# Two attention and two feed-forward layers on one core: gate and up weights on two queues, other weights behind them, wider fillers, another order

## The chip, the cores and the metric

The kernel runs on one core of one Trainium2 chip. The metric is the device time of one execution in microseconds (us). Engines named here: PE (TensorE, matrix multiplication), DVE (VectorE), ACT (ScalarE), POOL (GpSimd) and SP (SyncE, which here only issues transfers). Each engine runs its own list of instructions in order and waits on semaphores for the others. Transfers are issued from SP's list and from ACT's; the issue takes a place in that list, the data is moved by 16 DMA engines.

## The reference

A sequence of 2,048 tokens with 448 features, bf16, goes through four layers: attention, feed-forward, attention, feed-forward, each added to its input after a layer norm without weights. The same weights serve both pairs of layers.

```python
def _A_ref(x, wqkv, wo):            # 16 heads of 28
    W, dil = 8, 2
    q, k, v = ...                    # x @ wqkv
    idx = pos[:, None] - (jnp.arange(W) * dil)[None, :]   # 8 keys: own, and every second one before
    mask = idx >= 0
    logits = jnp.einsum("bhsd,bhswd->bhsw", q, kg) * scale
    attn = _softmax(jnp.where(mask, logits, -1e9))
    return einsum("bhsw,bhswd->bhsd", attn, vg) @ wo
def _B_ref(x, w_gate, w_up, w_down): # 448 -> 1792 -> 448, no nonlinearity
    return ((x @ w_gate) * (x @ w_up)) @ w_down
x = x + _A_ref(_layernorm(x), A_wqkv, A_wo)
x = x + _B_ref(_layernorm(x), B_w_gate, B_w_up, B_w_down)
# both lines once more
```

## The kernel before

x stays in SBUF (`x_sb`), 16 blocks of 128 tokens. The tokens are dealt to the blocks by parity, so that a step of two in the sequence is a step of one within a half. Work is cut into chunks of 256 or 512 tokens; a chunk of a layer is a job, and `SEQ` (line 77) lists the jobs: A00 is chunk 0 of attention layer 0, B10 chunk 0 of feed-forward layer 1, A2x and B3x are the second pair. Jobs of different layers overlap.

A chunk of attention: `ln_chunk` (771) computes bn_stats, the variance's logarithm and exponential on ACT, and the normalised block `xn_sb`. In layer 0 PE transposes it (line 812, copied to `xnTa` in line 818); in the later layers a DMA transpose on SP's queue does (805). `qk_chunk` (872) multiplies by `WQK` and copies the result to `qk` (904); four features per head group go through DRAM by seven small writes (913, `vt`) and come back by transposing loads (924), for all but the first tokens of layer 0. `v_group` (926) makes V. `attn_front` (1002) makes the scores (1016), their exponential (1023) and the mask (1033); `attn_back` (1041) multiplies by V (1053), and its result is evacuated (1064, 1068) and normalised (1078 to 1091). `y_blocks` (1095) multiplies by `wo_g` and `x_block` adds to x (1108).

A chunk of feed-forward, `b_chunk` (1118): for each of 14 column groups, seven steps with gate weights on partitions 0 to 63 and up weights on 64 to 127 of `WGU` side by side, a copy of the gate result on ACT (1144), the product on DVE (1147); then `WD` (twin_blocks, and 1159 for the last blocks) and the add. Nearly all matmuls are recorded by one helper and carry line 539, or 542 where four narrow strips replace a whole one, so that they can run between the matmuls of an attention product.

The order of each engine's list is not written by hand. `Sched` (136) takes every operation with an estimated duration, dependencies and a priority and simulates a list scheduler; what comes out is the order, and the waits are put in from it. Priorities are made of a job's place, of numbers per kind of operation (`PR`, `XP`) and per job (`JP`), and of `HEAD_P` for the first normalisations. `HOLD_A`, `HOLD_BA` and `HOLD_BB` say how long attention bursts are held back. `LINE_T`, `LINE_T2` and `LINE_W` are its assumption on how long PE takes to get 256 instructions. None of these numbers is on the chip; they change the order alone.

The first loads go out by `head_dma`: blocks of x on SP's queue, wqkv rows (into `hT`, used as a stage) on both. Until data is there PE multiplies zeros (line 705): `WARM` = 9 pairs of 512 columns, then `FILL` = 33 pairs of 256 with the lowest priority, which go wherever nothing else is ready. After the third group of x has landed (`BULK_AFTER`, the key ("x", -1, 8)) the bulk weights follow, all on SP's queue, by `bulk` (732): four loads of wo, eight of gate and up in turn (two halves of the columns, each in pieces of 4 and 3 of the 7 row groups, `KP`), and four of wd, the first after an evacuation of the first attention product, each other after the landing of the one before.

Of the kernel before, what the change touches and what calls it, by code (L numbers as in the profile page):

```python
# [27 lines left out]
MAIN = "R64"  # L28
# [2 lines left out]
MAXALT = 2  # L31
PE_T = ("00", "01", "02", "03", "04")
HEAD_LN = 5
HEAD_P = (-9741.69, -21156.5, 9471.13, 16516.09, 9510.52)
HOLD_A = 10125.5
HOLD_BA = 5146.2
HOLD_BB = 35088.1
HOLD_N = 2
S_EST = 288.0
AV_EST = 288.0  # L40
# [6 lines left out]
VT = 4  # L47
# [5 lines left out]
AVC = True  # L53
AVC_E = ("act", "dve")
NBK = 8
PR = {'AV': -13607.23, 'rstd': -12825.88, 'bn': -7069.68, 'N': -625.26, 'Gps': 7235.74, 'Tps': 2822.91, 'H': -12368.72, 'S': -4010.55, 'VT': 5090.9, 'Ex': 7210.49, 'G': 2122.84, 'xn': -11304.9, 'QK': 896.52, 'Ddps': 1031.01, 'V': 3968.38, 'x': 577.18, 'lnv': 7.22, 'Oc': 7676.01, 'Oa': -2117.27, 'R': 11367.91, 'VVps': -11282.71, 'Yps': -6204.95, 'PW': 15173.02, 'T': -4657.77, 'mv': -9765.28, 'Rs': 6778.63, 'Rl': -11802.58, 'QKps': -3286.81, 'E': -6014.8, 'wqk': -7832.24, 'wqp': 1681.38}
JP = {'A20': -5129.89, 'B32': -1640.88, 'B34': -20489.15, 'A22': -2226.98, 'B13': -11980.33, 'A21': -2482.24, 'B12': -12384.07, 'A02': 5531.08, 'A03': -2969.67, 'B30': -18200.21, 'B31': -1620.52, 'B10': -8375.7, 'B11': -7187.21, 'A23': -3100.22, 'A04': -7074.05, 'B33': 9501.01, 'A01': 4103.52, 'B14': -535.73, 'A00': 22844.77}
OFF = {}
XP = {'bn': -5669.71, 'mv': -13506.16, 'lnv': 1000.78, 'rstd': 5707.23, 'xn': 4967.8, 'Tps': -6347.24, 'T': -10883.81, 'QK': -8329.91, 'V': -3666.67, 'E': 818.94, 'Ex': -6364.37, 'S': -9748.38, 'AV': -5394.24, 'Oc': 7335.77, 'Oa': 10978.51, 'N': 720.48, 'x': -8291.39, 'VT': 14228.52, 'PW': 1447.12}
VONES_L = 6000.0  # L60
BL = (8000.0, 8000.0, 4800.0)
WOL = 3500.0
KP = ((0, 4), (4, 7))
BULK_Q = "sp"
BULK_WD = [("Oc", 0, 0, 0)]
BULK_AFTER = [("x", -1, 8)]
PAIR_PLAIN = (7, 7)
ACH = {0: (256, 512, 512, 512, 256), 2: (512, 512, 512, 512)}
BCH = {1: (256, 512, 512, 512, 256), 3: (256, 512, 512, 512, 256)}
WARM = 9  # L70
FILL = 33
SEED = 190
JITTER = 0
ATT_P = 17045.15
A_CAP = 6
B_CAP = 6
SEQ = "A00 A01 B10 A02 B11 A03 A04 B12 A20 B13 A21 B14 B30 A22 B31 A23 B32 B33 B34".split()
# [58 lines left out]
class Sched:  # L136
# [26 lines left out]
    def add(self, engs, ins, est, deps=(), prio=0.0, mode=None, acquire=None, release=(), dma=None, lat=0.0, after=None, selfd=(), tmin=None, alt=()):  # L163
# [78 lines left out]
    def run_pe(self, now, n, stream):  # L242

        n0 = self.fed[-1][0]
        t = now
        if self.fed[-1][1] < now:
            self.fed.append((n0, now))
        lead = min(self.QUEUE, (now - self.fed_at(n0, self.QUEUE)) / self.FETCH)
        end = now + stream
        if n > lead:  # L250
            end = max(end, now + (n - lead) * self.FETCH + self.REFILL)
        while len(self.lines) * self.LINE <= n0 + n + self.AHEAD:
            k = len(self.lines)
# [6 lines left out]
            self.lines.append(at + (self.LINE_T2 if self.LINE_W[0] <= at < self.LINE_W[1] else self.LINE_T))  # L260
# [25 lines left out]
    def schedule(self):  # L286
# [29 lines left out]
        while left:  # L316
            moved = False
            b_ready = any(o.acquire is not None and o.acquire.kind == 1 for o in pend["pe"])
            for e in self.ENGS:
# [28 lines left out]
                if okay and e == "pe":  # L348
# [219 lines left out]
def build(nc, A_x, A_wqkv, A_wo, B_w_gate, B_w_up, B_w_down, out):  # L568
# [52 lines left out]
    def one(fn, key=None):  # L621
        return [(fn, key)]
# [5 lines left out]
    def plain_dma(q, dst, src, key, sem, deps=(), lat=3000.0, prio=0.0, tmin=None):  # L628
        sc.add(q, one(lambda E: E.dma_start(dst, src), key), {"sp": 520.0, "act": 500.0, "pool": 1000.0}[q], deps=deps, dma=sem, mode=0, lat=lat, prio=prio, tmin=tmin)
# [72 lines left out]
    wb = Banks(2)  # L702
    fill = None
    for n in range(WARM + FILL):
        ins = [(lambda E, h=h, c=512 if n < WARM else 256: E.matmul(ps[:, wb[h], 0:c], warm[64 * h:64 * h + 64, 0:128], warm[64 * h:64 * h + 64, 0:c], start=True, stop=True), ("warm", n) if h else None) for h in range(2)]  # L705
# [21 lines left out]
    ones_dst = vt_all.rearrange("(t e) (a n) -> t e a n", e=32, n=128)[:, DH:32]  # L727
    ones_src = ones32[0:32, :].unsqueeze(1).to_broadcast([32, 16, 128])
    plain_dma("sp", ones_dst, ones_src, ("vones",), "d_one", deps=["c_ones"], lat=VONES_L, prio=-40)
    chain = []  # L730

    def bulk(dst, src, key, sem, lat):
        late = key[0] == "wd"
        deps = BULK_WD if late and key[1] == 0 else [chain[-1]] if late else BULK_AFTER
        plain_dma(BULK_Q, dst, src, key, sem, deps=["c_wo"] + deps, lat=lat, prio=-50.0 + len(chain) * 0.1)
        chain.append(key)

    for j in range(4):
        dst = wo_g[32 * j:32 * j + DH, :, :]
        src = A_wo.rearrange("(c j e) d -> j e c d", c=4, j=4, e=DH)[j]  # L740
        bulk(dst, src, ("wo", j), f"d_wo{j}", WOL)
    for n in range(2):
        f0, f1 = F // 2 * n, F // 2 * (n + 1)
        for m, (a, z) in enumerate(KP):
            for w, W_ in enumerate((B_w_gate, B_w_up)):
                bulk(WGU[64 * w:64 * w + 64, a:z, f0:f1], W_[64 * a:64 * z, f0:f1].rearrange("(k p) f -> p k f", p=64), (("wg", "wu")[w], n, m), f"d_w{'gu'[w]}{n}{m}", BL[0])
    for n in range(4):
        f0, f1 = (0, 4, 7, 11, 14)[n:n + 2]
        bulk(WD[:, f0:f1, :], B_w_down[128 * f0:128 * f1, :].rearrange("(c p) e -> p c e", p=128), ("wd", n), f"d_wd{n}", BL[2])
    WDR = [("wd", n) for n in range(4)]  # L750
    WO = [("wo", j) for j in range(4)]

# [365 lines left out]
    def b_chunk(li, j, n_b, prio):  # L1118
# [65 lines left out]
    def a_chunk(li, j, prio):  # L1184
# [105 lines left out]
```

## Time and profile before

| | |
|---|---|
| median of 3 runs (lowest, highest) | 392.72 us (392.54, 394.02) |
| profiled execution | 392.95 us |
| its span, first to last instruction | 391.2 us |
| PE busy | 381.8 us, 98% of the span |
| DVE, ACT busy | 272.8 us (70%), 204.6 us (52%) |
| granted TensorE clock | 1.000 |

The span is the time between the first and the last instruction of the profiled execution; 1.75 us of its time lie outside. In rows of the timeline stand the start and duration in us, the engine, the line of the kernel, the operation, the tiles written and read with their shapes, and the count; brackets give the idle time before it and what ended it. "PEld" is the loading of a matmul's weights, "SPq" and "ACTq" are transfers issued from these lists. In rows by stretch of time stand the length, then busy time and number of instructions for PE, PEld, DVE, ACT and POOL, then the granted clock, the share of time in which the 16 DMA engines are busy, and GB/s. Rows of transfers have their number, KB each and the median us from issue to landing. "issue" as a releaser means that the engine waited for nothing that the profile shows.

### The profile page before, as it was taken

Reading aid. Unit: us, or ns where it says so; the run is one execution under the profiler, and the core shown is the slowest. Engines: PE = TensorE matmul, PEld = TensorE weight load, DVE = VectorE, ACT = ScalarE, POOL = GpSimd, SP = SyncE. Lnnn points to the kernel's source line nnn. Section 1 sums busy time; section 2 is a strip of 40 time slices with the busy share of each in tenths; the row PEclk is TensorE's granted clock in tenths of the full one; section 3 lists DMA queues with packets and bytes.
Section 4 is the critical chain, followed back from the end, with each engine's and each line's share of the span. In section 5 each row is a group of like instructions: output and inputs, shape, how many; then the busy total and the mean of one; then the engine's idle time right before and its main releaser. Section 6 shows DMA issues by size and latency. Waiting matters only on the chain.

```text
span 391.2 us, 14452 instructions
## 1 busy us (share of the span) xinstructions
PE 381.8 (98%) x6416; PEld 215.3 (55%) x6416; DVE 272.8 (70%) x597; ACT 204.6 (52%) x394; POOL 8.9 (2%) x39
## 2 busy tenths in 40 slices
PE   8986999999999999999999999999999999999997
PEld 5644767754444445444556786455455544544584
DVE  5975799889997275645779972278768893466452
ACT  5886897848554221446854743157644732344150
POOL 7010000000000000000000000000000000000000
PEclk9999999999999999999999999999999999999999
DMA  8995331912210315411002115111214023100201
GB/s 273 240 219 130 72 55 23 88 20 49 49 30 1 50 29 85 80 34 26 8 3 51 29 30 96 35 23 24 55 26 72 27 47 49 50 3 2 52 23 47
DMA packets 54817, 22.50 MB, mean 58 GB/s; under 512 B 44948, under 2 KB 54756, under 8 KB 54756
## 3 DMA queue, kind: packets, MB, share of 16 engines
q1 hardware_dynamic: 54180, 20.85, 27.2%
q8 instruction: 50, 0.82, 0.9%
q10 hardware_dynamic: 576, 0.75, 0.6%
q14 instruction: 11, 0.09, 0.1%
HBM read 8.54 MB, written 2.71 MB: 29 GB/s over the span
## 4 chain that ended last, share of the span: by engine, by line
PE 90%; DVE 5%; ACT 2%; issue 1%; DMA 1%; DVEq 0%
PE ps L539 80%; PE ps L1016 3%; PE ps L705 2%; PE ps L1053 2%; PE ps L542 1%; PE ps L1159 1%; DVE x_sb L1108 1%; DMA xnTa<-xn_sb 1%; DVE st L781 1%; ACT qk L904 1%; ACT E_sb L1023 0%; DVE oT L1091 0%; DVE E_sb L1033 0%; ACT R_sb L1079 0%; DVE xn_sb L802 0%
## 5 line engine op out<-in xcount | busy, mean ns | idle before, releaser
L539 PE MATMUL ps<-xnTb,WGU 64*128 64x512 bf16 (+1 forms) x1926 | 175.5, 333 | 0.1
L539 PEld LDWEIGHTS ps<-xnTb,WGU 64*128 64x128 bf16 x1926 | 92.9, 94 | 70.7 <-issue 0.8
L1144 ACT ACTIVATE g_sb<-ps 128x512 bf16<-128x512 f32 (+1 forms) x140 | 71.0, 511 | 92.7 <-PE ps L539 85.9
L1147 DVE TENSOR_TENSOR hT<-g_sb,ps 128x512 bf16<-128x512 bf16 (+1 forms) x140 | 79.7, 575 | 37.1 <-ACT g_sb L1144 35.3
L539 PE MATMUL ps<-WD,hT 64*128 64x448 bf16 x836 | 84.1, 349 | 0.0
L1108 DVE TENSOR_TENSOR x_sb<-x_sb,ps 128x448 bf16<-128x448 bf16 x62 | 35.9, 615 | 37.1 <-PE ps L539 37.0
L539 PEld LDWEIGHTS ps<-WD,hT 64*128 64x128 bf16 x836 | 40.2, 94 | 36.8 <-DVE hT L1147 0.2
L539 PE MATMUL ps<-xnTa,WQK 64*128 64x512 bf16 (+1 forms) x492 | 51.5, 352 | 0.1
L1023 ACT ACTIVATE E_sb<-ps 128x1024 bf16<-128x1024 f32 (+1 forms) x36 | 33.8, 983 | 11.9 <-PE ps L1016 11.5
L781 DVE BATCH_NORM_STATS2 st<-x_sb 128x6 f32<-128x448 bf16 x64 | 37.9, 609 | 1.5 <-DMA x_sb<-in_A_x_dram 1.4
L539 PEld LDWEIGHTS ps<-xnTa,WQK 64*128 64x128 bf16 x492 | 23.2, 94 | 21.5 <-PE ps L539 1.1
L802 DVE TENSOR_SCALAR xn_sb<-x_sb,mv,rstd 128x512 bf16<-128x512 bf16 (+1 forms) x64 | 34.2, 569 | 0.8 <-ACT rstd L786 0.6
L904 ACT ACTIVATE qk<-ps 128x1024 bf16<-128x1024 f32 (+1 forms) x28 | 25.2, 902 | 17.3 <-PE ps L539 17.1
L1033 DVE TENSOR_TENSOR E_sb<-E_sb,MK 128x1024 bf16<-128x1024 bf16 (+2 forms) x40 | 24.0, 610 | 10.8 <-ACT E_sb L1023 10.8
L539 PE MATMUL ps<-wo_g,oT 64*128 64x448 bf16 x248 | 28.3, 349 | 0.3
L1091 DVE TENSOR_TENSOR oT<-O_sb,R_sb 128x480 bf16<-128x480 f32 (+3 forms) x36 | 21.9, 625 | 4.5 <-ACT R_sb L1080 4.3
L539 PE MATMUL ps<-WV,xnTa 64*128 64x336 bf16 (+3 forms) x252 | 23.1, 304 | 0.8 <-DMA xnTa<-xn_sb 0.7
L1078 DVE STREAM_SHUFFLE R_sb<-O_sb 128x480 f32<-128x480 f32 (+1 forms) x34 | 22.8, 694 | 0.0
L1079 ACT ACTIVATE R_sb<-R_sb 128x480 f32<-128x480 f32 (+1 forms) x34 | 20.2, 598 | 4.6 <-DVE R_sb L1078 4.6
L1064 ACT ACTIVATE O_sb<-ps 128x512 f32<-128x512 f32 (+3 forms) x24 | 12.7, 554 | 15.8 <-PE ps L1053 15.8
L1080 ACT ACTIVATE R_sb<-R_sb 128x480 f32<-128x480 f32 (+1 forms) x34 | 19.9, 601 | 0.4
L784 ACT ACTIVATE lnv<-mv,eps_sb 128x2 f32<-128x2 f32 (+1 forms) x33 | 9.6, 294 | 19.4 <-DVE mv L783 19.4
(57 smaller groups left out, 197.8 us busy)
## 6 DMA issues: line engine op xcount, KB each, us to landing
out_dram<-x_sb SPq DMA_DIRECT2D x15, 112.0 KB, 1.7
x_sb<-in_A_x_dram SPq DMA_DIRECT2D x3, 448.0 KB, 6.8
WGU<-in_B_w_gate_dram SPq DMA_DIRECT2D x2, 448.0 KB, 7.9
WGU<-in_B_w_up_dram SPq DMA_DIRECT2D x2, 448.0 KB, 9.2
WD<-in_B_w_down_dram SPq DMA_DIRECT2D x2, 448.0 KB, 6.2
hT<-in_A_wqkv_dram ACTq DMA_DIRECT2D x3, 224.0 KB, 3.4
WGU<-in_B_w_gate_dram SPq DMA_DIRECT2D x2, 336.0 KB, 10.1
WGU<-in_B_w_up_dram SPq DMA_DIRECT2D x2, 336.0 KB, 11.7
```

Source lines behind the costliest of these rows:

```text
L539: return lambda E: E.matmul(out(), lhs(), rhs(), start=start, stop=stop)
L781: sc.add("dve", one(lambda E, B=B: E.bn_stats(st6[:, B, :], x_sb[:, B, :]), ("bn", li, B)), 525.0, deps=[("x", li - 1, B)] + ([("xn", li - ...
L802: sc.add("dve", one(lambda E, B=B, dst=dst, src=src: E.tensor_scalar(dst, src, mv[:, B, 0:1], rstd[:, B:B + 1], ALU.subtract, ALU.mult), ( ...
L904: return E.activation(dst, src, ACT.Copy) if hasattr(E, "activation") else E.tensor_copy(dst, src)
L1023: return E.activation(E_sb[:, slot, 2 * hp:2 * hp + 2, 0:w], ps[:, b0:b0 + 2, 0:w], ACT.Exp, scale=SCALE)
L1033: return E.tensor_tensor(e, e, m, ALU.mult)
L1078: sc.add("dve", one(lambda E: E.stream_shuffle(R_sb[:, rs, 0:w], O_sb[:, os_, 0:w], [DH] * 32), ("Rs", li, qb)), dve_est(w) + 100.0, deps= ...
L1079: sc.add("act", one(lambda E: E.activation(R_sb[:, rs, 0:w], R_sb[:, rs, 0:w], ACT.Ln), ("Rl", li, qb)), act_est(w, False), deps=[("Rs", l ...
L1091: return E.tensor_tensor(oT[:, :, a % HALF:a % HALF + z - a], O[:, :, a - tok:z - tok], R_sb[:, rs, 0:w].rearrange("p (h n) -> p h n", h=4 ...
L1108: sc.add("dve", one(lambda E: E.tensor_tensor(x_sb[:, B, :], x_sb[:, B, :], ps[:, bk[w], 0:D], ALU.add), ("x", li, B)), dve_est(D), deps=[ ...
L1144: sc.add("act", one(lambda E, gs=gs, bk=bk: E.activation(g_sb[:, gs, 0:nt], ps[:, bk[0], 0:nt], ACT.Copy), ("G", li, j, fc)), act_est(nt), ...
L1147: sc.add("dve", one(lambda E, gs=gs, bk=bk, fc=fc: E.tensor_tensor(hT[:, fc, hs, 0:nt], g_sb[:, gs, 0:nt], ps[:, bk[1], 0:nt], ALU.mult), ...
```

## The change

The gate weights are now loaded by two transfers on SP's queue (one per half of the columns, all seven row groups), the up weights by two on ACT's queue. All four wait for the third group of x, as before, and go ahead of wo. The four loads of wo wait until the last up load has landed, the first load of wd waits for the last of wo, and each further one for the one before, all on SP's queue. The fillers of PE become 16 pairs of 512 columns instead of 33 of 256. The planner's numbers are new: priorities, hold times, estimated landing times (`BL`), and the assumed time for 256 instructions, which now depends on the time in four steps. With them the order of all lists is new; SP's first lists show it: gate x2, wo x4, wd, three vt writes, wd, four vt writes, wd, wd, seven vt writes, two transposes for feed-forward. On ACT's list the first up load stands behind the first copy of `qk`, the second between the two next `rstd`. In the attention layers the copies, transposes and bursts stand in other places; the last 60 us of PE's list are the same.

```diff
-HEAD_P = (-9741.69, -21156.5, 9471.13, 16516.09, 9510.52)
-HOLD_A = 10125.5
-HOLD_BA = 5146.2
-HOLD_BB = 35088.1
+HEAD_P = (38742.03, -267021.83, -101071.72, 99463.11, 27200.44)
+HOLD_A = 14413.3
+HOLD_BA = 5214.2
+HOLD_BB = 9573.3
...
-BL = (8000.0, 8000.0, 4800.0)
-WOL = 3500.0
-KP = ((0, 4), (4, 7))
-BULK_Q = "sp"
-BULK_WD = [("Oc", 0, 0, 0)]
+BL = (9000.0, 3500.0, 4000.0)
+KP = ((0, 7),)
...
-FILL = 33
+FILL = 16
...
-ATT_P = 17045.15
+ATT_P = 71709.67
...
-    LINE_T = 3500.0
-    LINE_T2 = 6500.0
-    LINE_W = (9000.0, 24000.0)
+    LINE_T = ((45000.0, 3500.0), (23000.0, 4600.0), (11000.0, 8500.0), (-1.0, 3500.0))
...
     for n in range(WARM + FILL):
-        ins = [(lambda E, h=h, c=512 if n < WARM else 256: E.matmul(...
-        sc.add("pe", ins, 428.0 if n < WARM else 109.0, deps=["c_warm"], mode=MAIN,
+        ins = [(lambda E, h=h, c=512: E.matmul(...
+        sc.add("pe", ins, 428.0 if n < WARM else 216.0, deps=["c_warm"], mode=MAIN,
...
-    chain = []
-
-    def bulk(dst, src, key, sem, lat):
-        late = key[0] == "wd"
-        deps = BULK_WD if late and key[1] == 0 else [chain[-1]] if late else BULK_AFTER
-        plain_dma(BULK_Q, dst, src, key, sem, deps=["c_wo"] + deps, lat=lat, prio=-50.0 + len(chain) * 0.1)
-        chain.append(key)
-
-    for j in range(4):
-        dst = wo_g[32 * j:32 * j + DH, :, :]
-        src = A_wo.rearrange("(c j e) d -> j e c d", c=4, j=4, e=DH)[j]
-        bulk(dst, src, ("wo", j), f"d_wo{j}", WOL)
+    def bulk(q, dst, src, key, sem, deps, lat):
+        sc.add(q, one(lambda E: E.dma_start(dst, src), key), {"sp": 520.0, "act": 500.0}[q], deps=["c_wo"] + deps, dma=sem, mode=0, lat=lat, prio=-300.0 + 0.1 * len(sc.ops) * (q == "sp"))
+        return key
+
     for n in range(2):
         f0, f1 = F // 2 * n, F // 2 * (n + 1)
         for m, (a, z) in enumerate(KP):
             for w, W_ in enumerate((B_w_gate, B_w_up)):
-                bulk(WGU[64 * w:64 * w + 64, a:z, f0:f1], ..., BL[0])
+                last = bulk(("sp", "act")[w], WGU[64 * w:64 * w + 64, a:z, f0:f1], ..., BULK_AFTER, BL[0])
+    for j in range(4):
+        dst = wo_g[32 * j:32 * j + DH, :, :]
+        src = A_wo.rearrange("(c j e) d -> j e c d", c=4, j=4, e=DH)[j]
+        prev = bulk("sp", dst, src, ("wo", j), f"d_wo{j}", [last], BL[1])
     for n in range(4):
         f0, f1 = (0, 4, 7, 11, 14)[n:n + 2]
-        bulk(WD[:, f0:f1, :], ..., ("wd", n), f"d_wd{n}", BL[2])
+        prev = bulk("sp", WD[:, f0:f1, :], ..., ("wd", n), f"d_wd{n}", [prev], BL[2])
```

The numbers in `PR`, `JP` and `XP` are all replaced, with a new entry for up (`wu`).

More of the change, by code (lines that the diff above doesn't have):

```diff
@@ L55 @@
 NBK = 8
-PR = {'AV': -13607.23, 'rstd': -12825.88, 'bn': -7069.68, 'N': -625.26, 'Gps': 7235.74, 'Tps': 2822.91, 'H': -12368.72, 'S': -4010.55, 'VT': 5090.9, 'Ex': 7210.49, 'G': 2122.84, 'xn': -11304.9, 'QK': 896.52, 'Ddps': 1031.01, 'V': 3968.38, 'x': 577.18, 'lnv': 7.22, 'Oc': 7676.01, 'Oa': -2117.27, 'R': 11367.91, 'VVps': -11282.71, 'Yps': -6204.95, 'PW': 15173.02, 'T': -4657.77, 'mv': -9765.28, 'Rs': 6778.63, 'Rl': -11802.58, 'QKps': -3286.81, 'E': -6014.8, 'wqk': -7832.24, 'wqp': 1681.38}
@@ L57 @@
-JP = {'A20': -5129.89, 'B32': -1640.88, 'B34': -20489.15, 'A22': -2226.98, 'B13': -11980.33, 'A21': -2482.24, 'B12': -12384.07, 'A02': 5531.08, 'A03': -2969.67, 'B30': -18200.21, 'B31': -1620.52, 'B10': -8375.7, 'B11': -7187.21, 'A23': -3100.22, 'A04': -7074.05, 'B33': 9501.01, 'A01': 4103.52, 'B14': -535.73, 'A00': 22844.77}
+PR = {'wu': -168129.17, 'AV': -10462.61, 'rstd': -35978.42, 'bn': 17812.95, 'N': -10212.21, 'Gps': 180828.64, 'Tps': 27409.69, 'H': -109807.89, 'S': 144044.56, 'VT': 70347.33, 'Ex': 79610.91, 'G': -13543.26, 'xn': -79108.55, 'QK': -38047.91, 'Ddps': 24073.96, 'V': -99754.84, 'x': -42794.27, 'lnv': -73394.18, 'Oc': -92185.76, 'Oa': -11984.14, 'R': 151556.02, 'VVps': -36455.43, 'Yps': 17459.84, 'PW': 63857.07, 'T': -30210.14, 'mv': -55530.81, 'Rs': -97577.45, 'Rl': 77935.78, 'QKps': 68347.44, 'E': 103540.24, 'wqk': -93887.3, 'wqp': 55786.95}
@@ L58 @@
+JP = {'A20': -91058.29, 'B32': 33273.33, 'B34': -254788.12, 'A22': -140282.28, 'B13': -13087.65, 'A21': -140403.13, 'B12': -98678.01, 'A02': 51851.79, 'A03': -34167.99, 'B30': -93145.7, 'B31': 78379.27, 'B10': -36992.85, 'B11': -174975.04, 'A23': -71630.68, 'A04': 3260.23, 'B33': -59282.63, 'A01': -61687.66, 'B14': 99825.17, 'A00': -37201.99}
 OFF = {}
-XP = {'bn': -5669.71, 'mv': -13506.16, 'lnv': 1000.78, 'rstd': 5707.23, 'xn': 4967.8, 'Tps': -6347.24, 'T': -10883.81, 'QK': -8329.91, 'V': -3666.67, 'E': 818.94, 'Ex': -6364.37, 'S': -9748.38, 'AV': -5394.24, 'Oc': 7335.77, 'Oa': 10978.51, 'N': 720.48, 'x': -8291.39, 'VT': 14228.52, 'PW': 1447.12}
+XP = {'bn': -95955.38, 'mv': 16148.21, 'lnv': -72635.24, 'rstd': 84849.74, 'xn': -172701.07, 'Tps': 15935.95, 'T': 8483.92, 'QK': 48768.14, 'V': -165679.11, 'E': 31912.32, 'Ex': -27261.18, 'S': 103908.79, 'AV': -35522.85, 'Oc': 78601.92, 'Oa': -68237.35, 'N': 141909.88, 'x': -106916.56, 'VT': 41247.37, 'PW': -72014.64}
@@ L259, in run_pe @@
             at = max(at, self.lines[-1])
-            self.lines.append(at + (self.LINE_T2 if self.LINE_W[0] <= at < self.LINE_W[1] else self.LINE_T))
+            self.lines.append(at + next(t for t0, t in self.LINE_T if at >= t0))
         k = (n0 + n) // self.LINE
@@ L704, in build @@
     for n in range(WARM + FILL):
-        ins = [(lambda E, h=h, c=512 if n < WARM else 256: E.matmul(ps[:, wb[h], 0:c], warm[64 * h:64 * h + 64, 0:128], warm[64 * h:64 * h + 64, 0:c], start=True, stop=True), ("warm", n) if h else None) for h in range(2)]
-        sc.add("pe", ins, 428.0 if n < WARM else 109.0, deps=["c_warm"], mode=MAIN,
+        ins = [(lambda E, h=h, c=512: E.matmul(ps[:, wb[h], 0:c], warm[64 * h:64 * h + 64, 0:128], warm[64 * h:64 * h + 64, 0:c], start=True, stop=True), ("warm", n) if h else None) for h in range(2)]
+        sc.add("pe", ins, 428.0 if n < WARM else 216.0, deps=["c_warm"], mode=MAIN,
                acquire=wb if n == 0 else None, release=[(wb, 0), (wb, 1)] if n == WARM + FILL - 1 else [], prio=-1e6 if n < WARM else 1e6, after=fill)
@@ L745, in build @@
             for w, W_ in enumerate((B_w_gate, B_w_up)):
-                bulk(WGU[64 * w:64 * w + 64, a:z, f0:f1], W_[64 * a:64 * z, f0:f1].rearrange("(k p) f -> p k f", p=64), (("wg", "wu")[w], n, m), f"d_w{'gu'[w]}{n}{m}", BL[0])
+                last = bulk(("sp", "act")[w], WGU[64 * w:64 * w + 64, a:z, f0:f1], W_[64 * a:64 * z, f0:f1].rearrange("(k p) f -> p k f", p=64), (("wg", "wu")[w], n, m), f"d_w{'gu'[w]}{n}{m}", BULK_AFTER, BL[0])
+    for j in range(4):
+        dst = wo_g[32 * j:32 * j + DH, :, :]
+        src = A_wo.rearrange("(c j e) d -> j e c d", c=4, j=4, e=DH)[j]
+        prev = bulk("sp", dst, src, ("wo", j), f"d_wo{j}", [last], BL[1])
     for n in range(4):
         f0, f1 = (0, 4, 7, 11, 14)[n:n + 2]
-        bulk(WD[:, f0:f1, :], B_w_down[128 * f0:128 * f1, :].rearrange("(c p) e -> p c e", p=128), ("wd", n), f"d_wd{n}", BL[2])
+        prev = bulk("sp", WD[:, f0:f1, :], B_w_down[128 * f0:128 * f1, :].rearrange("(c p) e -> p c e", p=128), ("wd", n), f"d_wd{n}", [prev], BL[2])
     WDR = [("wd", n) for n in range(4)]
```

## The prediction

> **What bounds the kernel now.** First the page's shares of the span, then who the matmul engine (PE) waited for, then its timeline where the longest wait lies.
>
> ```profile
> span 391.2 us, 14452 instructions
> PE 381.8 (98%) x6416; PEld 215.3 (55%) x6416; DVE 272.8 (70%) x597; ACT 204.6 (52%) x394; POOL 8.9 (2%) x39
> ...
> PE ps L1053 <- issue: 3.0, 1, 3.0
> PE ps L705 <- DVE eps_sb L669: 1.3, 1, 1.3
> PE ps L539 <- DMA xnTa<-xn_sb: 0.7, 1, 0.7
> PE ps L1016 <- ACT xnTa L818: 0.7, 1, 0.7
> ```
>
> PE is busy for 381.8 of 391.2 us, so the time is its work plus its waits, and the change keeps that work: counted in the two built programs, matmuls other than fillers differ only by twelve more, which come from splitting one more group into narrow strips. What can move is the waits. One of 3.0 us stands out; those of DVE and ACT are a quarter of it. Its place:
>
> ```profile
> 22.77 0.52 PE L1053 MATMUL ps<-E_sb,v_sb 64*32 64x72 bf16 x32
> ...
> 24.24 0.71 PE L1016 MATMUL ps<-qk 28*64 28x64 bf16 x64 [0.70 <-ACT xnTa L818]
> 24.88 4.08 PE L539 MATMUL ps<-xnTa,WQK 64*128 64x512 bf16 x34
> ...
> 31.94 0.26 PE L1053 MATMUL ps<-E_sb,v_sb 64*32 64x64 bf16 x16 [2.97 <-issue]
> ...
> 37.20 0.29 PE L812 MATMUL ps<-ident,xn_sb 64*128 64x64 bf16 x8 [0.30 <-ACT v_sb L996]
> ...
> q8 instruction: 50, 0.82, 0.9%
> ```
>
> PE stands still from 28.97 to 31.94 and waits for no engine ("issue"). In the program that place is matmul 474; each matmul is a weight load and a multiplication, so about 950 instructions lie before it. Queue q8 brings instructions: 50 packets for 6416 + 6416 PE instructions are 257 each. PE stops some 70 instructions before the fourth multiple of 256: I read it as waiting for a block of 256 instructions, fetched when PE enters the block ahead (an estimate from these rows). Here are the DMA engines at that time, by stretches of 4 us (the last two columns are their busy share and GB/s), and q8 between 29 and 30 us:
>
> ```profile
> 8.00:12.00 4.00, 4.00 (x84) 3.46 (x80) 4.00 (x13) 2.27 (x7) 1.98 (x9) 1.00 1.10 355
> 12.00:16.00 4.00, 3.92 (x112) 2.87 (x108) 3.70 (x13) 3.74 (x13) 0.00 (x0) 1.00 0.77 206
> 16.00:20.00 4.00, 3.93 (x36) 1.59 (x37) 4.00 (x15) 3.38 (x9) 0.00 (x0) 1.00 1.07 216
> 20.00:24.00 4.00, 3.54 (x94) 1.94 (x90) 3.71 (x12) 3.52 (x8) 1.20 (x6) 1.00 1.07 215
> 24.00:28.00 4.00, 3.69 (x92) 1.84 (x94) 3.39 (x10) 3.73 (x7) 0.00 (x0) 1.00 1.07 219
> 28.00:32.00 4.00, 1.03 (x26) 0.38 (x24) 0.69 (x1) 2.02 (x3) 0.00 (x0) 1.00 0.91 187
> ...
> q8 instruction: 1, 0.02, 8.4%
> ```
>
> The engines are full from 16 to 31 us, with the gate and up weights. The block that PE needs at 28.97 is moved only between 29 and 30. The edge before it (70 instructions before 768) is matmul 347, in the row at 22.77, so this fetch took 31.94 - 23 = 9 us under load. With idle engines it takes no more than 5.3: the edge after it (matmul 601) is in the transposes about 37.2, and the 0.30 there are ACT's.
>
> **The change, part by part.**
>
> *Gate on SP's queue, up on ACT's, in two pieces each, ahead of the wo weights.* The loads that now fill the engines:
>
> ```profile
> L629 SPq DMA_DIRECT2D WGU<-in_B_w_gate_dram x4: 612/616/722, 12.9 to 16.9; - x4
> L629 SPq DMA_DIRECT2D WGU<-in_B_w_up_dram x4: 611/614/617, 13.6 to 17.6; - x4
> ...
> DMA to landing us min/median/max: 5.0/10.0/14.1
> ...
> WGU<-in_B_w_gate_dram SPq DMA_DIRECT2D x2, 448.0 KB, 7.9
> WGU<-in_B_w_gate_dram SPq DMA_DIRECT2D x2, 336.0 KB, 10.1
> ...
> 10.05 2.76 SPq L629 DMA_DIRECT2D wo_g<-in_A_wo_dram  x4
> ```
>
> Gate and up are 4 x 448 + 4 x 336 KB = 3.2 MB. On one queue they move at 216 GB/s, and the last lands at 17.6 + 14.1 = 31.7 us. Each piece goes to 64 partitions only (gate to 0-63, up to 64-127, by the code), while the x and wv loads before 12 us, to all 128, moved at 355. With the two halves on two queues at the same time the rate lies between 216 and 355. Without the 2.76 us of wo issues ahead, they start at 10 us; what is queued before them keeps the engines until about 12. At 355 GB/s they are in at 12 + 9 = 21 us, at 216 at 27. I take 355, since both halves are then in flight and 128 partitions are the nearest row.
>
> By the Trainium skill, page "SBUF — State Buffer", section "Can I just issue two DMAs to hit both halves?", two DMAs at partitions 0 and 64 measured only 6% over one. By it the weights would be in at about 26 us, and the sum would be that of the first rival, 392.4; its port rule (64 partitions reach half of the ports, some 218 GB/s) agrees with the 216 above. No run here shows yet which holds for two queues.
>
> What this does to PE: in the new program the block edges, placed alike, are matmuls 219, 345 and 472. Between the last two lie 5 of the attention product, 64 scores, 52 QK matmuls of 256 columns and 6 of 512. Durations:
>
> ```profile
> 103.90 9.17 PE ps L539 x84
> ...
> 59.49 0.64 PE ps L1016 x64
> ...
> 40.97 2.47 PE L539 MATMUL ps<-xnTa,WQK 64*128 64x256 bf16 x42
> ```
>
> So 0.05 + 0.64 + 52 x 0.055 + 6 x 0.109 = 4.2 us, against about 4.6 before: the fetch has no more time than before. If the weights are in at 21, the block wanted at edge 472 is fetched from about 24 on idle engines, in at most 5.3 us: wait 0 to 1.1, and since 5.3 is a ceiling I take 0. The 2.97 us go. If they are in at 27, the wait stays between 1 and 3.
>
> *ACT issues the two up loads*, right after its first QK copy and between the two rstd of the next blocks.
>
> ```profile
> 0.85 1.34 ACTq L629 DMA_DIRECT2D hT<-in_A_wqkv_dram  x3
> ...
> 13.13 0.60 ACT L904 ACTIVATE qk<-ps 128x512 bf16<-128x512 f32 x1 [0.18 <-PE ps L539]
> ...
> 15.59 0.34 PE L1016 MATMUL ps<-qk 28*64 28x72 bf16 x32
> ```
>
> An issue costs ACT 1.34 / 3 = 0.45 us, or 0.61 by SP's rows for these weights: 0.9 to 1.2 us, in a stretch where ACT is busy for 3.74 of 4 us. Behind them wait one rstd, so two normalised blocks, and three QK copies of 0.60 us, so the first scores (15.59). The new order puts eight V matmuls, 8 x 0.095 = 0.76 us of PE's work, behind those scores, so waiting for them costs that much sooner. Ends: 0 and +1.2. I take +0.5: ACT has 0.26 us to spare there, and PE still has other blocks' transposes to do.
>
> *Fillers.* 33 pairs of 256 columns become 16 pairs of 512.
>
> ```profile
> 1.26 6.35 PE L705 MATMUL ps<-hT 64*128 64x512 bf16 x48 [1.26 <-DVE eps_sb L669]
> ...
> 8.12 1.36 PE L705 MATMUL ps<-hT 64*128 64x256 bf16 x22
> ```
>
> A late pair of 256 takes 1.2 / 11 = 0.11 us, so of 512 0.22: 33 x 0.11 = 3.6 against 16 x 0.22 = 3.5 us. Up to 9.3 us PE waits for x and its normalisation anyway; a coarser filler can hold back a transpose by at most 0.2. I take +0.1. The 34 matmuls fewer move the block edges, which is counted above.
>
> *wo behind the landing of the last up load, the first wd load behind that of wo, on SP's queue (the other wd loads waited for each other before, too).* Behind these waits stand 14 vt writes and the first transposes for the feed-forward layer.
>
> ```profile
> WD<-in_B_w_down_dram SPq DMA_DIRECT2D x2, 448.0 KB, 6.2
> WD<-in_B_w_down_dram SPq DMA_DIRECT2D x2, 336.0 KB, 3.5
> ...
> 46.89 2.68 SPq L805 DMA_TRANSPOSE xnTb<-xn_sb  x2
> ```
>
> From weights in at 21: wo issued until 24, in at about 27, then four loads of some 4 us end near 44, and the seven vt writes between cost little. The transposes are wanted not much before 46.9, so the cost is 0. With weights in at 27 the chain ends near 50 and costs up to 3. First uses (wo at about 34 us, wd past 60) are covered in the first case.
>
> *New order and hold times.* They move whole groups; the page shows few waits behind 80 us. Two places become tighter, below (second rival). I take 0: the old wait of 0.7 for xnTa goes or is replaced.
>
> Sum against the profiled execution of 392.95 us: - 2.97 + 0.5 + 0.1 + 0 + 0 = - 2.4, so 390.6. Its time is 0.23 above the median of 392.72, so the forecast is 390.4.
>
> **The rivals.**
>
> *The halves take turns, and nothing is gained.* For it: one queue at a time already fills the engines (share 1.07). Against it: full engines at 216 GB/s beside 355 at the same share say that the target, not the engine, is slow. Weights in at 27: the wait of 2.97 becomes about 2, ACT's 0.5 is added, SP's chain costs some tenths: 390.6 + 2 - 0.2 = 392.4. It is decided by when the last up load lands: after 25 us it holds.
>
> *A wait for xnTa in the second attention layer takes its place: slower.* The chain of waits has this piece now:
>
> ```profile
> 203.06 1.14 DVE x_sb L1108 x2
> ...
> 216.25 4.06 DMA xnTa<-xn_sb
> 220.35 37.86 PE ps L539 x492
> ```
>
> From the residual add at 203.06 to the V matmuls at 220.35 it takes 17.3 us, and PE waited 0.7 of them. In the new order the same V matmuls (query block 10) stand behind fewer: 42 WD matmuls, 64 scores and 140 WGU matmuls of 256 columns, so 42 x 0.095 + 0.64 + 140 x 0.055 = 12.3 us. If the chain takes as long there, PE waits 5 us, and the time is 395.4. Against it: much of the 17.3 is DVE doing other things in between. It decides from a chain of 16.6 us on (4.3 above 12.3 would make the change slower).
>
> **How the numbers follow.** What can be told from no change is 0.5%, 1.96 us: faster is under 390.76, slower over 394.68. The forecast's case, weights in early and the wait gone, has 0.50 (387.8 to 391.8: ACT's term from 0 to 1.2, other waits 2 less or 0.5 more), of which 0.40 are faster. The first rival has 0.25 (391.5 to 393.8), all within the bound. The second has 0.17, of it 0.15 slower. The rest, 0.08, is a new order that loses or wins elsewhere: 0.03 faster, 0.05 slower. Sums: faster 0.43, same 0.37, slower 0.20. The range reaches from 387.8 to 395.2, with about 1 in 10 on either side.
>
> **What would show it.** The last up load lands by 22 us; the DMA rate from 12 to 20 us is over 300 GB/s; "issue" is gone from PE's waits over 1 us; PE reaches the first paired attention product before 30 us instead of at 31.94. ACT's part is right if the first scores start between 15 and 16.5. The prediction is wrong if the weights land after 25, if PE waits over 1 us for instructions before 35, or if a wait for xnTa or xnTb of more than 1.5 us appears.

## The result, and the profile after

The changed kernel takes 390.73 us in the median of 8 runs (390.29 to 392.05); the kernel before took 392.83 beside it (8 runs). The ratio is 0.9947, with an interval of 0.9927 to 0.9967. Two repeats of the unedited kernel, below, gave 390.46 and 390.70; all 27 runs have a median of 390.64. The forecast was 390.4. The main term of its sum, the wait that goes, came out right, though the landing time from which it was worked out did not; the cost of the new order, put at nothing, was missing. That the time came so near is partly luck: other terms were too high by about as much.

First the page and PE's waits of the changed kernel (waits: line, what it waited for, us in total, times, longest). The profiled execution took 392.05 us, the longest of the eight.

```profile
span 390.3 us, 14405 instructions
PE 381.5 (98%) x6394; PEld 213.8 (55%) x6394; DVE 275.9 (71%) x606; ACT 200.8 (51%) x386; POOL 8.3 (2%) x38
...
PE ps L1044 <- issue: 1.7, 2, 1.0
PE ps L700 <- DVE eps_sb L664: 1.3, 1, 1.3
PE ps L534 <- issue: 0.8, 1, 0.8
PE ps L1007 <- ACT E_sb L1014: 0.6, 1, 0.6
PE ps L803 <- ACT qk L895: 0.5, 2, 0.3
```

PE's work is the same. The one wait of 3.0 us is gone; in its place stand three of 0.8 to 1.0, also for "issue". Where they lie, in PE's timeline of the changed kernel:

```profile
15.12 0.34 PE L1007 MATMUL ps<-qk 28*64 28x72 bf16 x32
...
29.20 0.15 PEld L1044 LDWEIGHTS ps<-E_sb,v_sb 64*32 64x32 bf16 x21 [0.21 <-issue]
29.21 0.27 PE L1044 MATMUL ps<-E_sb,v_sb 64*32 64x64 bf16 x21
...
42.06 0.71 PE L1007 MATMUL ps<-qk 28*64 28x64 bf16 x64 [0.62 <-ACT E_sb L1014]
50.92 0.22 PE L1044 MATMUL ps<-E_sb,v_sb 64*32 64x64 bf16 x7 [0.96 <-issue]
54.98 1.69 PE L534 MATMUL ps<-xnTb,WGU 64*128 64x256 bf16 x27 [0.77 <-issue]
72.54 0.24 PE L1044 MATMUL ps<-E_sb,v_sb 64*32 64x64 bf16 x12 [0.77 <-issue]
```

The paired attention product that the kernel before reached at 31.94, PE now reaches at 29.21, with a wait of 0.21 in the row of its weight loads. So 2.7 us are won by 30 us, and part is given back between 40 and 73. In the repeat, whose profiled execution has a span of 388.7, the wait near 51 us is 0.68 and the one near 54 is 0.20.

How the weights came in: the changed kernel by stretches of 2 us (last column GB/s), and the share of the two queues in two of these stretches (q1 carries gate, q10 up).

```profile
12.00:14.00 2.00, 1.61 (x44) 1.22 (x40) 1.95 (x6) 1.92 (x6) 0.00 (x0) 1.00 1.04 260
14.00:16.00 2.00, 1.86 (x62) 0.96 (x61) 2.00 (x9) 1.25 (x3) 0.00 (x0) 1.00 1.07 203
16.00:18.00 2.00, 2.00 (x22) 0.94 (x20) 2.00 (x7) 1.97 (x8) 0.00 (x0) 1.00 1.06 217
18.00:20.00 2.00, 1.92 (x46) 1.14 (x40) 1.82 (x7) 1.84 (x4) 0.00 (x0) 1.00 1.05 299
20.00:22.00 2.00, 1.89 (x18) 0.81 (x20) 1.91 (x5) 1.73 (x5) 0.00 (x0) 1.00 1.06 358
22.00:24.00 2.00, 1.86 (x62) 1.02 (x56) 1.63 (x9) 1.47 (x2) 0.50 (x3) 1.00 1.08 288
24.00:26.00 2.00, 1.52 (x87) 1.35 (x82) 1.43 (x6) 2.00 (x6) 0.59 (x4) 1.00 0.38 83
```

```profile
q10 hardware_dynamic: 223, 0.39, 102.1%
q1 hardware_dynamic: 10, 0.02, 4.8%
...
q10 hardware_dynamic: 202, 0.36, 52.4%
q1 hardware_dynamic: 204, 0.34, 49.8%
```

The first pair is 14 to 16 us, the second 20 to 22. All four loads were issued by 13.3 us, but until about 18 one queue had the engines nearly to itself, at 203 to 217 GB/s, as on one queue before. Only then did the two run side by side, at 358. From 24 us on the engines are mostly free (share 0.38), while the last bytes trickle in: the last up load landed at 25.6 us (the wo loads, which wait for it, go out at 25.62), the last gate load at 26.6 (issued at 11.8, landed 14.8 later). That is past the 25 at which the prediction called itself wrong, and nearer to the 27 of the first rival than to the 21 of the forecast.

### The profile page after: what moved, and what is told of

Read it like the earlier page. It is cut to its first block, busy times and chain, and to the rows that moved or that the text cites. A ratio compares the mean times of both kernels' runs of the same rounds, so it can differ in the third digit from the quotient of the medians.

```text
span 390.3 us, 14405 instructions
## 1 busy us (share of the span) xinstructions
PE 381.5 (98%) x6394; PEld 213.8 (55%) x6394; DVE 275.9 (71%) x606; ACT 200.8 (51%) x386; POOL 8.3 (2%) x38
## 4 chain that ended last, share of the span: by engine, by line
PE 93%; ACT 4%; DVE 2%; issue 1%; ACTq 0%; DVEq 0%
PE ps L534 83%; PE ps L1007 3%; PE ps L1044 2%; PE ps L700 2%; PE ps L537 2%; PE ps L1150 1%; ACT qk L895 1%; ACT xnTa L809 1%; ACT E_sb L1014 1%; ACT R_sb L1070 0%; ACT g_sb L1135 0%; DVE oT L1082 0%; ACT O_sb L1055 0%; DVE v_sb L987 0%; DVE R_sb L1069 0%
## 5 line engine op out<-in xcount | busy, mean ns | idle before, releaser
L534 PEld LDWEIGHTS ps<-xnTb,WGU 64*128 64x128 bf16 x1942 | 94.2, 94 | 72.1 <-issue 1.5
L534 PE MATMUL ps<-WD,hT 64*128 64x448 bf16 x824 | 81.8, 349 | 0.0
L895 ACT ACTIVATE qk<-ps 128x1024 bf16<-128x1024 f32 (+1 forms) x30 | 26.9, 923 | 10.5 <-PE ps L534 10.3
L534 PE MATMUL ps<-wo_g,oT 64*128 64x448 bf16 x252 | 29.3, 349 | 0.1
L1055 ACT ACTIVATE O_sb<-ps 128x512 f32<-128x512 f32 (+3 forms) x22 | 11.5, 547 | 26.4 <-PE ps L1044 26.3
L534 PE MATMUL ps<-WV,xnTa 64*128 64x336 bf16 (+3 forms) x244 | 21.1, 304 | 0.2
L534 PEld LDWEIGHTS ps<-wo_g,oT 64*128 64x128 bf16 x252 | 12.5, 94 | 11.8 <-DVE oT L1082 1.1
```

The lines of the kernel that those rows point to most:

```text
L534: return lambda E: E.matmul(out(), lhs(), rhs(), start=start, stop=stop)
L895: return E.activation(dst, src, ACT.Copy) if hasattr(E, "activation") else E.tensor_copy(dst, src)
```

## The experiments

The theory (A, or 1, in the expectations): PE gets its instructions in packets of 16 KB on queue q8 (50 packets, 0.82 MB), each for about 127 matmuls (a weight load and a multiplication each); a packet is taken to be asked for when PE passes the edge one block ahead of it, and to queue behind the bulk weights, so what counts in the change is the loads, and of them the time at which the engines are free. The rivals: the second queue itself is what helps, whatever the time of landing; or the new order and the fillers bring the gain, or take part of it. Edits to the loads were made in the finished lists, so that all other instructions keep their order.

**The new order and fillers with the old sequence of loads, and the old order with the new one.**

```diff
 # a_oldbulk: the changed kernel, and on SP's list
+wo first, then gate and up in turn (four whole loads), all after the third group of x;
+first wd after ("Oc", 0, 0, 0), as before
```

> The new order and fillers, and the bulk loads as in the kernel before: wo first, then gate and up in turn, all on SP's queue (in four pieces of seven row groups), wd behind the first evacuation of attention. Theory A: weights in at 28 to 32 us, PE waits 1 to 3 us for instructions near 29 us; no issue on ACT (- 0.5); 391.5 to 393.5, ratio 0.997 to 1.002. Theory B (order): as the changed kernel or faster by ACT's part, 389.8 to 390.8, ratio 0.992 to 0.995.

```diff
 # b_newbulk: the kernel before, and
-eight pieces of gate and up on SP, behind wo
+gate (2 loads) on SP; up (2) on ACT, after ("QK", 0, 0, 0) and after ("rstd", 0, 4)
+wo behind the last up load, first wd behind wo
```

> The old order of everything, and only the bulk loads as in the changed kernel: gate in two pieces on SP's queue, up in two on ACT's, wo behind the last up load, wd behind wo. Theory A (the loads' earlier end takes away PE's wait for instructions at 29 us): weights in near 25 us, the wait of 2.97 falls to 0 to 1, the two issues on ACT cost 0 to 1; time 390.3 to 392.0, ratio 0.994 to 0.998. Theory B (the gain is in the new order): no gain or a loss by ACT's issues, 392.8 to 394, ratio 1.000 to 1.003.

a_oldbulk: 396.82 us, ratio 1.0103 (1.0079 to 1.0126). b_newbulk: 389.52, ratio 0.9917 (0.989 to 0.9943), below the 390.3 to 392.0 of its theory. So the loads alone bring the whole gain and more; the new order without them loses 4 us. For a_oldbulk the theory (391.5 to 393.5) had the reason but by far not the size. PE's waits and stretches of a_oldbulk show why (third column from the right: the granted clock):

```profile
PE ps L534 <- issue: 4.4, 2, 4.2
PE ps L1044 <- issue: 1.9, 2, 1.1
```

```profile
24.00:32.00 8.00, 4.90 (x127) 3.53 (x126) 5.24 (x14) 5.41 (x13) 0.48 (x3) 1.00 1.07 203
...
33.00:34.00 1.00, 0.14 (x2) 0.13 (x3) 0.00 (x0) 0.00 (x0) 0.00 (x0) 0.88 0.34 95
34.00:37.00 3.00, 3.00 (x89) 1.59 (x88) 0.00 (x0) 1.56 (x3) 0.00 (x0) 0.50 0.06 17
37.00:38.00 1.00, 1.00 (x12) 0.51 (x10) 0.85 (x5) 1.00 (x2) 0.00 (x0) 0.92 0.61 128
```

The loads start later there and end at 32.6 us, the wait grows to 4.2, and after it PE runs at half its clock for some 3.4 us, which costs about half of that, 1.7 us.

**One queue for gate and up, with wo and wd still behind them**, in the new order and in the old one.

```diff
 # a_onequeue (changed kernel), b_onequeue (b_newbulk)
-up on ACT's list
+up on SP's list, each behind its gate load
```

> The changed kernel with its two up loads on SP's queue, each behind its gate load; wo and wd behind them as in the changed kernel. Theory A with the two halves side by side on two queues as the cause: one half at a time moves at 216 GB/s, weights in at 27 to 28 us instead of 25.5, wait near 29 us 1 to 2.5, ACT free of two issues (- 0.5): 391 to 392.7, ratio 0.996 to 1.000. Rival C (it is wo and wd that had to go, the second queue gives nothing): weights in by 26, no wait, 389.9 to 390.7, ratio 0.992 to 0.995.

> The old order and fillers; gate and up whole (four loads) in turn on SP's queue, ahead of wo and wd as in the changed kernel. If only the time at which the engines are free again counts: weights in at 28 to 29 us as in a_onequeue, the instruction packet between 27.5 and 28.7, PE goes on about 2.8 us later, so 30.3 to 31.5 instead of 31.94: wait 1.6 to 2.9, and 391.5 to 392.6. If what counted was wo and wd behind and not the second queue: no wait over 0.6 near 29 us, 389.5 to 390.5.

a_onequeue: 392.73 us, ratio 1.0002 (0.9982 to 1.0021), with a wait of 2.0 us, both as the theory has it. b_onequeue: 393.46, ratio 1.0015 (0.9994 to 1.0037), above its expectation. Taking wo and wd out of the way brings nothing by itself in the old order (393.46 against 392.83 before); in the new order it brings 4.1 us (392.73 against the 396.82 of a_oldbulk, whose wait of 4.2 becomes 2.0), so much that the new order is then no worse than the old one. The second queue is worth another 2.1 us in the new order (392.73 against 390.64), and 3.7 in the old (393.46 against 389.77, the 14 runs of b_newbulk and its repeat). PE's timeline of b_onequeue:

```profile
23.85 0.28 PE L1053 MATMUL ps<-E_sb,v_sb 64*32 64x72 bf16 x21 [1.20 <-issue]
31.37 0.28 PE L1053 MATMUL ps<-E_sb,v_sb 64*32 64x64 bf16 x21 [2.32 <-issue]
```

The wait at 31.37 fits the theory (expected 1.6 to 2.9). What was not expected is the one at 23.85: the packet before it is late too. b_onequeue then has the half clock as well (0.50 from 33 to 35 us).

**Half of the bytes later, on the old queue, in the old order.**

```diff
 # b_spread: the kernel before, and on SP's list
-second column halves of gate and up behind the first
+their four pieces between the wd loads: one after wd1, two after wd2, one after wd3
```

> The order, the fillers and the one queue of the kernel before; only the second column halves of the gate and up weights (four pieces, 1.57 MB) are issued later, one at a time between the WD pieces. Theory 1 (the instruction block that PE waited for until 31.94 us stood behind the bulk bytes, on whichever queue): the weights issued early are in by about 23 us, the wait of 2.97 us falls under 0.5; the late pieces may cost waits of up to 1 us in all between 36 and 50 us. 389.5 to 391.5 us. Theory 2 (the gain needs the second queue, or both partition halves at once): the wait stays and the time is 392.5 to 393.2.

391.06 us, ratio 0.9957 (0.9935 to 0.9979; eight of the nine runs from 389.57 to 392.96, one 395.50 at a clock of 0.991). PE's timeline of b_spread has no wait for instructions at 29 us any more, and others when the late pieces move:

```profile
39.80 1.05 PE L539 MATMUL ps<-xnTa,WQK 64*128 64x256 bf16 x16 [0.26 <-issue]
...
43.67 0.58 PE L1016 MATMUL ps<-qk 28*64 28x64 bf16 x49 [0.93 <-issue]
```

The wait goes with one queue and one partition half at a time. That is the time of the theory (389.5 to 391.5) and not of its rival (392.5 to 393.2): the second queue is not needed for it, and helps because it has the bytes out of the way sooner.

The trace's list of packets on the instruction queue, set beside PE's matmuls at the block edges, shows the same for every kernel (us; "asked" is when PE passes matmul 347, in the new order 346; "moved" the start of the packet; "idle" PE's wait before matmul 474, in the new order 473, and "goes on" the start of that matmul):

```
kernel       bulk bytes end  asked  moved   idle  goes on
before             30.5      23.0   29.2    2.97    31.9
a_oldbulk          32.6      24.7   31.0    4.18    33.9
b_onequeue         29.4      23.9   28.9    2.32    31.4
a_onequeue         30.0      24.7   28.5    1.98    31.7
changed            26.1      23.8   25.4    0       28.9
b_newbulk          26.0      23.1   24.2    0       28.5
b_spread        (pause 23)   22.9   23.6    0       29.0
```

With the engines full for all of that time the packet starts 3.8 to 6.3 us after it is asked for, else 0.7 to 1.6; from its start PE, where it waits for it, needs 2.4 to 3.2 us more. In the four kernels that wait it starts 0.5 to 1.6 us before the last bulk bytes, so it does not stand behind all of them. The edge is the same matmul in all kernels of one order.

**Fillers.** Narrow fillers in the changed kernel, wide ones in b_newbulk; PE's time in them is the same, only the number of matmuls ahead of all other work changes by 32.

```diff
 # a_fill256: changed kernel
-16 pairs of 512 columns
+32 pairs of 256
 # b_newfill: b_newbulk
-33 pairs of 256
+16 pairs of 512, one of 256
```

> The changed kernel with its 16 pairs of 512-column fillers as 32 pairs of 256: the same PE time, 32 matmuls more, so every later instruction block begins 32 matmuls earlier in the work. If the wide fillers are what makes the changed kernel about 0.9 us slower than its loads in the old order: 389.5. If the new order is: 390.2 to 390.8, less or more what the moved block edges do to the waits for instructions near 51, 54 and 72 us (0.7 to 1.7 us in all in two profiles), so 389.5 to 391.2 at the outside, and these waits are found at other instructions.

> The old order with the changed kernel's loads (389.5), and 32 of its 33 filler pairs merged two by two into pairs of 512 columns. If fillers cost nothing: 389.2 to 389.8, with the waits for instructions (0.46 at 23.1 us, 0.64 at 42.5, 0.28 at 75.7) moved or changed by the block edges, which lie 32 matmuls later in the work. If wide fillers hold back the first transposes and are the 0.9 us: 390.2 to 390.6.

a_fill256: 391.03 us, ratio 0.9952 (0.9933 to 0.9972): as the changed kernel. Its waits near 51 us, from PE's timeline, stand at matmuls 981 and 1108, as in the changed kernel (981 and 1107), though the work there is another by 32 matmuls:

```profile
52.42 0.23 PE L1045 MATMUL ps<-E_sb,v_sb 64*32 64x64 bf16 x10 [0.85 <-issue]
56.38 0.32 PE L1008 MATMUL ps<-qk 28*64 28x64 bf16 x30 [0.90 <-issue]
```

So it is the count of instructions that sets these waits. b_newfill: 391.42 us, ratio 0.9977 (0.9945 to 1.001), in two groups, six runs from 389.17 to 390.05, all at a clock of 1.000, and six from 392.80 to 394.77, all at 0.991 or 0.996. Width costs nothing in the first group; the profile of one of the second shows what the moved edges can do (timeline, then stretches):

```profile
45.99 0.28 PE L1016 MATMUL ps<-qk 28*64 28x64 bf16 x17 [3.61 <-issue]
```

```profile
42.00:46.00 4.00, 0.39 (x49) 0.28 (x30) 2.18 (x4) 0.75 (x4) 0.00 (x0) 1.00 0.63 155
46.00:50.00 4.00, 4.00 (x37) 1.61 (x39) 1.87 (x4) 1.94 (x2) 0.00 (x0) 0.57 0.39 77
```

Between matmuls 728 and 855 PE there has only 2.1 us of work (40.3 to 42.4), and the packet for the next block starts 3.4 us after it is asked for, at 43.7. The engines are not full then (share 0.2 to 0.6 from 40 to 42.5). A wd load is issued at 40.80, its packets run from about 41.6 to 43.7, and the instruction packet starts as they end; so this load may be what holds it, but that was not tried.

**Cut by row groups.**

```diff
 # c_rows: b_newbulk
-two loads each of gate and up: halves of the columns, 7 row groups
+two loads each: 2 and 5 of the 7 row groups, all columns
```

> The old order with the changed kernel's queues, but gate and up cut by row groups (2 and 5 of 7) over all columns instead of by columns: packets of 3584 bytes instead of 1792, and a first piece of 0.45 MB. If a partition half alone is limited by its packets: over 300 GB/s from the first piece, the weights in by 20 us, the wait at 23.1 us (0.46) gone, 388.8 to 389.4. If it is limited by bytes: still about 205 to 220 GB/s while one queue runs alone, both together from about 15 us instead of 18.5, the weights in by about 23, 389.2 to 389.6.

390.95 us, ratio 0.9954 (0.9934 to 0.9973): 1.2 us slower than b_newbulk's 389.77 (interval 0.7 to 2.1, from drawing the runs again at random), against both expectations. Packets of 3584 bytes, mostly on one queue at a time, moved at 210 to 229 GB/s from 14 to 20 us, so twice the packet size does not raise that rate. Both queues ran side by side from 20 us on only, and the last up load landed at 27.8, 1.1 us later than in b_newbulk. What waits behind it on SP's list comes later too: the first transposes for feed-forward go out at 47.53 instead of 43.69. Its profile has a wait of 1.30 us at 64.95 for DVE (`hT`) that b_newbulk does not have; whether the later transposes caused it was not tried.

**Repeats of the two best.** No edit.

> The kernel of b_newbulk unedited, beside the changed kernel on the same chip. If the new order costs something that the old one does not (blocks of instructions that PE uses up in 2.6 and 3.0 us near 47 and 51 us, while a fetch takes 3.6 to 4.1 without load): 389.2 to 389.8, and 0.6 to 1.3 below the changed kernel. If the first 389.52 was chance: 390.3 to 390.9, as the changed kernel.

> The changed kernel unedited: 390.3 to 390.9, granted clock 1.000 in every run, the wait for instructions at the edge near 51 us between 0.6 and 1.1.

b_newbulk_again: 389.84 us, ratio 0.9919 (0.9892 to 0.9946), 0.9 below after_third, as expected if the first was no chance. after_third: 390.70, ratio 0.9947 (0.9922 to 0.9971); its time was as expected, the rest was not: one of the twelve runs had a clock of 0.995 (394.35 us), and the wait near 51 us was 0.39. The first repeat of the changed kernel, beside b_newbulk:

> The changed kernel once more, unedited, for a second profile. In the first one PE waits three times for 0.77 to 0.96 us with 'issue' (at 50, 54 and 72 us) and the execution takes 392.05 us, 1.3 above the median of 390.73. Theory A (PE waits for blocks of 256 instructions where the DMA engines are busy): these waits differ from execution to execution; a profile near the median shows fewer or shorter ones, and none above 1 us before 45 us. Theory B (the order alone sets the waits): the same three waits again. Ratio to the kernel before 0.9947, between 0.993 and 0.997, under both.

390.46 us, ratio 0.9938 (0.9915 to 0.996), with fewer and shorter waits (0.68 and 0.20), as theory A has it. Over all runs the changed kernel's loads in the old order (14 runs, 389.77) are 0.9 us faster than the changed kernel (27 runs, 390.64), and the best of all that ran; the difference has an interval of 0.4 to 1.6, from drawing the runs again at random. The stretches 12 to 20, 40 to 50 and 50 to 60 us of before, after_again and b_newbulk, one fence each (first number after the length: PE busy):

```profile
12.00:20.00 8.00, 7.85 (x146) 4.46 (x142) 7.70 (x26) 7.11 (x20) 0.00 (x0) 1.00 0.92 211
40.00:50.00 10.00, 9.78 (x310) 6.97 (x304) 8.70 (x18) 8.90 (x16) 0.00 (x0) 1.00 0.40 86
50.00:60.00 10.00, 9.87 (x271) 6.64 (x258) 9.91 (x23) 8.84 (x16) 0.00 (x0) 1.00 0.23 40
```

```profile
12.00:20.00 8.00, 7.54 (x166) 4.64 (x160) 7.80 (x25) 6.78 (x17) 0.00 (x0) 1.00 1.05 251
40.00:50.00 10.00, 9.09 (x321) 5.10 (x319) 7.13 (x16) 8.71 (x13) 0.00 (x0) 1.00 0.67 128
50.00:60.00 10.00, 9.11 (x236) 7.66 (x221) 9.00 (x22) 8.68 (x16) 0.00 (x0) 1.00 0.19 35
```

```profile
12.00:20.00 8.00, 7.87 (x142) 4.37 (x139) 7.75 (x26) 7.21 (x21) 0.00 (x0) 1.00 1.05 225
40.00:50.00 10.00, 9.14 (x324) 5.23 (x317) 8.51 (x19) 8.63 (x17) 0.00 (x0) 1.00 0.46 103
50.00:60.00 10.00, 9.80 (x289) 6.93 (x270) 10.00 (x24) 8.91 (x15) 0.00 (x0) 1.00 0.16 28
```

Against b_newbulk the new order loses 7.87 - 7.54 = 0.33 us of PE's time between 12 and 20 and 9.80 - 9.11 = 0.69 between 50 and 60. The second is where the waits for instructions stand: there PE has 2.8 us of work between matmuls 855 and 981 (47.2 to 50.0 in the changed kernel) and 3.3 between 981 and 1107 (50.9 to 54.2), while from one edge to the use of the packet asked for there it took 3.6 to 4.1 us in waits of this kind (changed kernel 50.92 to 54.98, b_newbulk 38.91 to 42.48, b_spread 39.80 to 43.67; gate and up were in by then, but for b_spread's). It can be less: in the kernel before, PE passed such edges at 42.38 and 45.14 without waiting. Why a packet starts at once in one execution and 1 to 3 us late in another was not settled.

These waits do not make up the 0.9, though. PE's waits for instructions in the changed kernel (after_again), then in b_newbulk:

```profile
PE ps L1044 <- issue: 0.7, 1, 0.7
PE ps L1007 <- issue: 0.2, 1, 0.2
```

```profile
PE ps L1016 <- issue: 0.9, 2, 0.6
PE ps L1053 <- issue: 0.5, 1, 0.5
```

In all that is 0.9 us (0.6 in after_third) against 1.4 (0.8 in b_newbulk_again): the old order has such waits too, at 23, 42 and 75 us. Only the first profile of the changed kernel, of its longest run, has 2.5.

Part of the loss between 12 and 20 is ACT's. In the new order the same matmuls run with ACT issuing the up loads (changed kernel) and without (a_oldbulk, a_onequeue). PE's timeline of a_oldbulk and of after_third, from a group of QK matmuls to the first scores:

```profile
11.31 0.94 PE L534 MATMUL ps<-xnTa,WQK 64*128 64x256 bf16 x14
...
15.01 0.34 PE L1007 MATMUL ps<-qk 28*64 28x72 bf16 x32
```

```profile
11.68 0.94 PE L534 MATMUL ps<-xnTa,WQK 64*128 64x256 bf16 x14
...
14.00 0.29 PE L803 MATMUL ps<-ident,xn_sb 64*128 64x64 bf16 x8 [0.28 <-ACT qk L895]
...
16.20 0.34 PE L1007 MATMUL ps<-qk 28*64 28x72 bf16 x32
```

Without the issues this takes 3.7 us (a_oldbulk) and 3.9 (a_onequeue), with them 4.2, 4.0 and 4.5 in the three profiles of the changed kernel: 0.1 to 0.8 more, 0.4 in the mean. In the third the second issue took 1.09 us instead of 0.60.

## Why the prediction came out as it did

*The wait of 2.97 us goes: right, though not by the stated arrival, and so in part by luck.* It went from 2.97 to 0.21, and b_newbulk, which has the loads and nothing else of the change, gains 392.83 - 389.77 = 3.06. Not all of that need be the wait itself: of 72 executions of the kernel before that ran beside the experiments, 30 show a mean clock of 0.995 or 0.996 (median 393.03 us), as one stretch of 3.4 us at half clock would give, and 42 show 1.000 (392.44), while b_newbulk shows 1.000 in all 14. The reading of the "issue" wait as a block of instructions behind the bulk bytes held in every kernel of the table. What failed in this step is "I take 355, since both halves are then in flight": the halves were in flight together from 18 us only, the rate from 12 to 20 was 203 to 299 and not over 300, and the last up load landed at 25.6, not by 22. By the prediction's own sign ("wrong if the weights land after 25") the wait should have stayed. It went all the same, since the engines were mostly free from 24 us on, before the last bytes were in: the block was asked for at 23.8, moved from 25.4, and was needed at 28.9. So the first rival's rule "after 25 us it holds" was too strict: with 2.4 to 3.2 us from packet to use, a packet started by about 26 is in time for 28.9.

*ACT's two issues, +0.5: about right.* Measured between 11 and 16 us it is 0.1 to 0.8, 0.4 in the mean. It is a cost of the new order only: b_newbulk has the issues at 10.2 and 11.9 us, and PE is as busy from 12 to 20 as before (7.87 and 7.85). The sign given for it, first scores between 15 and 16.5, tells nothing: they start at 15.12 in the changed kernel and at 15.01 in a_oldbulk, which has no such issues.

*Fillers, +0.1: nothing by their width* (six runs of b_newfill from 389.17 to 390.05, b_newbulk 389.77; a_fill256 as the changed kernel). That "the 34 matmuls fewer move the block edges, which is counted above" was counted at one edge only; b_newfill shows that 32 matmuls fewer can make a wait of 3.6 us elsewhere, in some executions.

*wo and wd on SP, 0: right.* The transposes for the feed-forward layer go out at 45.42 and PE waits for none of them; the last two wd loads are issued between 38.7 and 42.6.

*The new order, 0: the step that failed.* The changed kernel is 0.9 us above b_newbulk; with some 0.4 of that for ACT, about 0.5 is left for the new order, an estimate that is no better than the interval of the 0.9 (0.4 to 1.6). "The page shows few waits behind 80 us" looked past the stretch from 40 to 73, and the places searched were those where data comes late. There the new order puts small matmuls closer together, and PE waits for blocks of instructions near 51 and 54 us. But the old order has as much waiting of this kind at other places, so the cause of the 0.5 stays open.

The sum as measured is - 3.1 + 0.4 + 0 + 0 + 0.5 = - 2.2 where - 2.4 stood: the new order's term was too low by 0.5, and the other terms together too high by 0.3. *The second rival did not occur:* no wait for xnTa or xnTb over 0.5 us stands in PE's list, and PE is busy for 40.00 of 40 us from 200 to 240. That the halves take turns, the first rival, was true for the first 6 us of the transfer and not after.

## What to carry to other kernels

In these kernels a PE that waited for "issue" at fixed instruction counts was waiting for its program. Where you meet such waits, look at the packets of the instruction queue and at what fills the DMA engines when PE passes the edge before, and move the bulk bytes out of that stretch or have them in sooner. Then look for blocks of instructions that hold less work than a fetch takes (2.1 to 3.3 us against 3.6 to 4.1 here), since a new order or a few matmuls more in front can make such a block or remove it. When a part costs nothing in one order, as ACT's issues here, that does not show what it costs in another. Try the parts of a change alone: here the loads alone were better than the whole.

## What the runs showed of the hardware that was not expected

Two queues to the two partition halves are neither in turn nor side by side from the start: the queue whose packets come first has the engines for about 4 us, then the other for 2 (203 to 217 GB/s each), and then both together at 358. Which is first changes: up in one profile of the changed kernel, gate in its repeat. The Trainium skill, page "SBUF — State Buffer", section "Can I just issue two DMAs to hit both halves?", has +6% for two such transfers. The stretch from 20 to 22 us has 358 against 217 from 16 to 18, 65% more; here the measurement decides, and the page's "they serialize" fits the first 6 us only.

A wait of 2 to 4 us can cost more than itself. After waits of 4.2 (a_oldbulk), 3.6 (b_newfill), 2.3 (b_onequeue) and 2.0 us (a_onequeue) PE's granted clock was 0.50 for about 3.4 us, some 1.7 us of lost work; after 2.97 us in the profile of the kernel before it stayed at 1.00, though 30 of that kernel's 72 other executions show a mean clock under 1.000. The Trainium skill, page "TensorE: Matmul & The Clock Gate", section "Part 1: The HAM clock gate (the "warmup" mystery)", gives the half rate after an idle window of about 3.4 us and the same time to come back; the trace agrees on the half and on the time back, but 2.0 us of idling were enough, and 2.97 once were not.
